# A delta-rule recurrence with a soft mixture of experts on one core: output tokens stored in runs of 20 a partition, 64-row remainders side by side, one urgency offset for each operation

## The chip, the cores and the metric

One core of a Trainium2 chip runs the whole program. The metric is the device time of one execution in microseconds. Three executions of the kernel before took 446.22, 451.45 and 451.5 us, median 451.45.

## The reference

```python
for t in range(S):                       # 4 batches, 8 heads, S = 768, D = 40
    y[:, :, t] = einsum('bhd,bhde->bhe', rt, state)
    Sa = einsum('bhde,bhe->bhd', state, at)
    state = state * wt[:, :, None, :] - einsum('bhd,bhe->bhde', Sa, bt)
    state = state + einsum('bhd,bhe->bhde', vt, kt)
x = y.transpose(0, 2, 1, 3).reshape(3072, 320)
logits = x @ phi                         # 32 slots, 4 for each of 8 experts
d = softmax(logits over the tokens)
slot_input = d.T @ x
for e in range(8):                       # w1[e]: 320 x 1024, w2[e]: 1024 x 320
    slot_out[e] = relu(slot_input[e] @ w1[e]) @ w2[e]
out = softmax(logits over the slots) @ slot_out
```

## The kernel before, in words

The sequence is cut into 12 steps of 64 tokens (`NST`), two of which make one superstep of 128. The 32 pairs of batch and head stand in three units (`u`) of 3, 3 and 2 heads. For a step, the decays `ww` are multiplied up by two scans on VectorE (`scan_s`, `scan_c`), which give the factors for `kb` (`scan_k`) and for `aa` (the product `ahs`). ScalarE spreads `ahs` into a block-diagonal matrix (`bd_mult`, for the first steps; later ones load it), with the mask column `bm_t`. `lgram` and `gram` multiply it with the keys on TensorE and mask the results. For each superstep a triangular matrix is inverted (`solve_in`, 30 `solve_step`, `solve_out`) by VectorE and GpSimd; it begins and ends with a transpose of 128 x 1024 on VectorE. With the inverse, `chain_g`, `chain_u` and `chain_s` carry the state from step to step, which is the serial part; `y_vut`, `y_sd`, `y_p` and `y_y` give the outputs `xs`. `slots_a` to `slots_e` turn them into logits, running maxima and sums, and the slots' inputs, which `merge_m` and `merge_s` finish as `sit`.

Then come the experts. In the first layer each output bank (experts 4g to 4g+3, half f of the 1024 columns) is filled by three passes over the 320 inputs: two of 128 rows and a remainder of 64 rows, four experts beside each other in the four column tiles of 32. ScalarE applies the ReLU, TensorE transposes, VectorE copies into `ht`. The second layer (`second`, 64 matmuls of 160 columns for each half of the output columns) adds into one bank. Its result is split into two float32r parts, combined by `sel_r`, and cast to `s4`. The last matmuls multiply the softmax over the slots, transposed by `stack` for each superstep, with `s4`: in groups of three, 160 columns each. ScalarE and VectorE copy the results out in turns, and SP stores them. Before, a partition holds token t of a step, so each run in memory is half a token's row, 640 bytes; the second half of the columns is computed while the first is stored.

No order is written out. Every call is recorded as an operation (`Plan.record`), with its cost by rules (`pe_cost`, `costs`), and `forward` lets each engine take, of the operations that are ready, the one with the highest urgency: the longest way to the end of the program, plus an offset. Before, the offsets are the sum of 32 random patterns (`noise`, `SEEDS`). Where the plan has TensorE wait over 0.9 us, `fill` puts filler matmuls, which stand under L550 (128 rows) and L554 (32 rows) in the profile. `pace` lets a transfer wait for an earlier one where over 500 KB would be in flight (`PACE`). All other planned instructions stand under one line, L1273 (L1276 after the change; the fillers under L553 and L557). In the profile `wt` stands for eight large tiles that the weights `in_w` share with the recurrence, `mem`, `old` and `mid` for smaller ones, `cs_t` for the constants.

## Time and profile before

| What | Value |
|---|---|
| median of three executions | 451.45 us (446.22 to 451.5) |
| span of the profiled execution | 443.0 us |
| median above that span | 8.45 us |
| busy: TensorE, VectorE, GpSimd, ScalarE | 376.9, 267.3, 242.8, 221.3 us |
| HBM read, written | 54.01 MB, 3.93 MB |

The page gives the profiled execution's span, from its first to its last instruction, and not its whole time; the fastest of the three executions is 3.2 us above this span. In a row of the timeline stand the start, the duration, the engine, the operation with its tiles and shape, and in brackets the idle time ahead of it with what ended it. A float32 matmul leaves two records. In the rows by stretches a pair of numbers is busy time and number of instructions.

### The profile page before, as it was taken

The numbers are of one execution on the slowest core, as the hardware profiler recorded it, in microseconds if no ns is written. First come the engines' busy times: TensorE is split into PE (matmuls) and PEld (weight loads), VectorE is DVE, ScalarE is ACT, GpSimd is POOL, SyncE is SP. The second block draws the span as 40 slices with busy tenths as digits, with TensorE's granted clock in tenths as the row PEclk, the third lists the DMA queues.
The fourth block names the chain that finished last, engine by engine and source line by source line (L and its number), as shares of the span: only waits on it lengthen the run. The fifth ranks groups of instructions, "written<-read, shape, count | busy, mean of one in ns | idle before, by whom it ended". The sixth has DMA issues, their size and how long they took to land.

```text
span 443.0 us, 21393 instructions
## 1 busy us (share of the span) xinstructions
PE 376.9 (85%) x9411; PEld 317.3 (72%) x9411; DVE 267.3 (60%) x554; ACT 221.3 (50%) x633; POOL 242.8 (55%) x410
## 2 busy tenths in 40 slices
PE   0497998998999899789998999989899887899900
PEld 0487997787978789678986789868787576537800
DVE  6869999789965377854479555646354542522400
ACT  1630364774555564957449854697257535202310
POOL 3838884897288964788976889278810000200000
PEclk9999999999999999999999999999899989979965
DMA  8997023135322334613446315585557835870276
GB/s 203 260 237 221 8 65 101 31 90 135 84 72 77 108 82 119 166 43 94 114 127 184 98 44 148 156 249 179 157 151 211 254 105 156 251 218 1 60 164 134
DMA packets 42206, 59.33 MB, mean 134 GB/s; under 512 B 4785, under 2 KB 32545, under 8 KB 42113
## 3 DMA queue, kind: packets, MB, share of 16 engines
q1 hardware_dynamic: 42113, 57.96, 47.3%
q8 instruction: 74, 1.21, 1.2%
q14 instruction: 19, 0.16, 0.1%
HBM read 54.01 MB, written 3.93 MB: 131 GB/s over the span
## 4 chain that ended last, share of the span: by engine, by line
PE 66%; DVE 8%; ACT 7%; DMA 6%; issue 4%; POOL 3%; SPq 1%; ACTq 0%; POOLq 0%; DVEq 0%
PE ps L1273 60%; DVE wt L1273 7%; ACT wt L1273 6%; POOL wt L1273 3%; PE ps L550 3%; PE ps L554 3%; DMA wt<-in_kb_dram 3%; DMA wt<-in_ww_dram 1%; DMA wt<-in_w_dram 1%; DVE mem L1273 1%; DMA wt<-in_aa_dram 1%; SPq L1273 1%; ACT mem L1273 1%; DMA wt<-in_rr_dram 0%; ACT mid L1273 0%
## 5 line engine op out<-in xcount | busy, mean ns | idle before, releaser
L1273 POOL TENSOR_TENSOR wt<-wt 128x30 f32<-128x30 f32 (+23 forms) x360 | 177.5, 493 | 58.7 <-ACT wt L1273 32.8
L1273 PE MATMUL ps<-wt,wt 128*32 128x40 f32 (+8 forms) x4200 | 134.3, 224 | 10.1 <-ACT wt L1273 4.0
L1273 PEld LDWEIGHTS ps<-wt,wt 128*32 128x32 f32 (+6 forms) x4200 | 114.4, 118 | 25.1 <-issue 8.1
L1273 DVE TENSOR_TENSOR wt<-ps,cs_t 128x384 f32<-128x384 f32 (+5 forms) x132 | 64.1, 498 | 49.3 <-PE ps L1273 39.0
L1273 PE MATMUL ps<-cs_t,wt 120*128 120x120 f32 (+5 forms) x496 | 69.0, 273 | 15.5 <-DMA cs_t<-in_consts_dram 13.3
L1273 ACT ACTIVATE wt<-ps 32x120 f32<-32x120 f32 (+1 forms) x288 | 70.1, 249 | 19.3 <-PE ps L1273 13.2
L1273 POOL TENSOR_TENSOR wt<-wt,wt 120x768 f32<-120x768 f32 x32 | 56.6, 1779 | 24.7 <-DVE wt L1273 8.7
L1273 ACT COPY wt<-ps 128x120 f32<-128x120 f32 (+3 forms) x116 | 38.9, 354 | 61.4 <-PE ps L1273 57.0
L1273 PEld LDWEIGHTS ps<-cs_t,wt 120*128 120x128 f32 (+5 forms) x496 | 52.2, 140 | 21.9 <-issue 14.8
L1273 PE MATMUL ps<-wt,mem 128*32 128x160 f32 (+4 forms) x592 | 65.2, 313 | 1.1 <-ACT mem L1273 0.4
L1273 ACT COPY mem<-ps 120x480 f32<-120x480 f32 (+6 forms) x99 | 45.0, 480 | 40.9 <-PE ps L1273 32.1
L1273 PEld LDWEIGHTS ps<-wt,mem 128*32 128x32 f32 (+4 forms) x592 | 52.5, 153 | 4.6 <-ACT mem L1273 1.6
L1273 DVE TENSOR_TENSOR_SCAN wt<-wt,wt 120x780 f32<-120x780 f32 x24 | 43.0, 1793 | 3.9 <-DMA wt<-in_ww_dram 2.1
L1273 DVE TENSOR_TENSOR wt<-wt 128x27 f32<-128x27 f32 (+25 forms) x100 | 41.4, 414 | 2.1
L1273 PE MATMUL ps<-mem 32*32 32x40 f32 (+2 forms) x1040 | 33.9, 232 | 3.4 <-issue 1.9
L1273 DVE TENSOR_TENSOR ps<-ps,wt 120x480 f32<-120x480 f32 (+1 forms) x30 | 18.1, 606 | 29.8 <-PE ps L1273 27.7
L1273 ACT ACTIVATE wt<-wt,bm_t 120x768 f32<-120x768 f32 (+1 forms) x36 | 28.5, 858 | 10.6 <-PE ps L1273 4.1
L1273 POOL MEMSET mem<- 128x2048 f32 x1 | 1.8, 1805 | 57.5 <-DVE mid L1273 57.5
L550 PE MATMUL ps<-cs_t 128*128 128x128 f32 x218 | 27.1, 280 | 1.1 <-ACT mem L1273 1.1
L1273 PE MATMUL ps<-wt 32*32 32x40 f32 x1536 | 24.6, 201 | 3.3 <-issue 1.3
L1273 ACT COPY wt<-wt 120x768 f32<-120x768 f32 (+5 forms) x20 | 16.5, 836 | 21.4 <-DVE wt L1273 18.8
L550 PEld LDWEIGHTS ps<-cs_t 128*128 128x128 f32 x218 | 25.6, 194 | 1.6 <-ACT mem L1273 1.3
(89 smaller groups left out, 323.1 us busy)
## 6 DMA issues: line engine op xcount, KB each, us to landing
wt<-in_w_dram SPq DMA_DIRECT2D x16, 640.0 KB
wt<-in_kb_dram SPq DMA_DIRECT2D x36, 240.0 KB
wt<-in_w_dram SPq DMA_DIRECT2D x16, 512.0 KB
wt<-in_ww_dram SPq DMA_DIRECT2D x12, 366.6 KB
...
```

Of the source, the lines that this page charges most:

```text
L550: self.nc.tensor.matmul(bank, src, src, start=True, stop=True)
L554: self.nc.tensor.matmul(bank[i:i + 32], src[r, 0:32], src[r], start=True, stop=True)
L1273: nc.vector.memset(one_f, 0.0)
```

## The change

Four things change together.

1. `stack` writes the transposed softmax of the first five supersteps into one tile `cst_old` of 2,560 columns, in the order batch, step, token. The last matmul takes every 20th column of it (`src[:, r::nr]`), so that partition q gets tokens 20q to 20q + 19; the last superstep gives 4 consecutive tokens a partition. A token's 320 columns come in one matmul, one copy for each, and a store moves 2 to 6 tokens of 32 partitions in runs of 2,560 to 7,680 bytes (24 stores; before, 20). Both halves of the second layer are therefore computed ahead of the first output, and `more`, which mixed them, is gone.
2. The loop over the first layer has `f` outside. Two banks (g = 0, 1) take the 128-row passes, then both remainders follow as one operation (`gather`): `w1_load` puts the remainders of experts 4 to 7 into the other half of the partitions, so that the eight matmuls stand in eight different tiles of 64 rows by 32 columns.
3. The offsets come from a table with one character for each operation (`SHIFT`).
4. The planner's costs: 16 array tiles for the matmuls instead of 4 columns, and the start of a matmul operation by kind (`START`) instead of 170; an operation may need two banks.

```diff
@@ -37,9 +37,8 @@
             ba=(0.824, 1.778), lw=(0.869, 1.012), br=(0.72, 0.82), s0=(0.643, 1.33))
 KV = 3
 BM, AV = NST, 2
-OX = ((1, 3, 7), (3, 7))
-OXG = ()
-FIN = dict(st=(0.03, 0.429), pos=(6, 0, 1), warm=(0, 0, 1, 1, 0, 1, 0, 0, 2, 0, 0), ms=(5, 2), l2=(6, 2, 3))
+OX = (2, 5, 10, 16, 20)
+FIN = dict(st=(0.03, 0.429), pos=(6, 0, 1), warm=(0, 0, 1, 1, 0, 1, 0, 0, 2, 0, 0), ms=(5, 2))
...
+START = ((225, 210), (195, 195))
 ROUNDS = 0
-SEEDS = (3, 21, 44, 62, 119, 136, 146, 166, 184, 236, 383, 839, 894, 1144, 1277, 1468, 1487, 1602, 1732, 2303, 3675, 4128,
-         4356, 4549, 5379, 5493, 5729, 5909, 5921, 5968, 6052, 6159)
-SPARE = 3
...
+STEP = {**{chr(79 + v): v for v in range(-44, 46)}, "~": 13, "!": -45}
+SHIFT = (
+    r"To')E:@oFhXL;s4JO+UO>!OQ!i0IXai!OO0zcwufU0#!2HOO,:!JPOTvYRS|N~[;tR7NkW~!7z]u2Hzu_O&B|%~!R_gLQOXOS#!OF|CO:H6NNQ!c"
...
+)
...
-            if o.mode == mode and isinstance(out, VAP) and o.banks == {out.bank} and o.tag == self.tag:
+            if o.mode == mode and isinstance(out, VAP) and (o.banks == {out.bank} or self.gather and o.gather) and o.tag == self.tag:
                 new = False
...
-            o.occ = self.pe_add(o, cost, lane) + 170
+            o.occ = self.pe_add(o, cost, lane) + START[method == "transpose"][mode[1] < 128]
...
-        for o, x in zip(self.ops, sum((self.noise(n) for n in SEEDS), 0 * self.noise(0))):
-            o.prio += x
+        for o, c in zip(self.ops, "".join(SHIFT)):
+            o.prio += 300 * STEP[c]
...
@@ -680,7 +683,8 @@
             for k in range(2):
                 nc.sync.dma_start(wv[:, 2 * p + k], w1[2 * i + p, 128 * k:128 * k + 128])
         for p in range(2):
-            nc.sync.dma_start(wv[64 * p:64 * p + 64, 4], w1[2 * i + p, 256:320])
+            o = 64 * ((p + i // 2) % 2)
+            nc.sync.dma_start(wv[o:o + 64, 4], w1[2 * i + p, 256:320])
 
     def w2_load(i, p):
         wv = wts[4 + i].rearrange("p (e j c) -> p e j c", e=2, c=HD)
@@ -1195,8 +1199,7 @@
             nc.vector.tensor_tensor(xv[:, :, 2:4], cb, xv[:, :, 0:2], ALU.subtract)
             for j in range(4):
                 nc.tensor.transpose(tp[:, 128 * j:128 * j + 128], x[:, 128 * j:128 * j + 128], ident)
-            t = cst_t[i] = stk[i]
-            (nc.vector.tensor_copy if i % 2 else nc.scalar.copy)(t, tp)
+            (nc.vector.tensor_copy if i % 2 else nc.scalar.copy)(stk[i], tp.rearrange("p (a b t) -> p a b t", a=2, t=C))
 
         mg = {}
 
@@ -1371,7 +1374,9 @@
                 w2_load(0, 1)
                 w2_load(1, 0)
         i = NSS - 1
-        stk += old_later([512] * (NSS - 1))
+        cst_old = old_later([512 * (NSS - 1)])[0]
+        ov = cst_old.rearrange("p (b s t) -> p b s t", b=B, t=C)
+        stk += [ov[:, :, 2 * k:2 * k + 2].rearrange("p b a t -> p a b t") for k in range(NSS - 1)]
         run_all(*y_lists(NST - 1, WIN), ([lambda k=k: slots_a(i, k, 0) for k in range(3)], .3, .6),
                 (one(lambda: stack(0)) + one(lambda: stack(1)), *FIN["st"]))
         w2_load(1, 1)
@@ -1385,7 +1390,7 @@
             seq.insert(x, lambda k=k: stack(k))
         for k, f in enumerate(seq):
             f()
-    rnd = mid_later([512, 256, 320, 320, 160, 160])
+    rnd = mid_later([512, 256, 320, 320, 320])
     w1s = [t.rearrange("p (a f) -> p a f", f=FF) for t in wts[:4]]
     w2s = [t.rearrange("p (e j c) -> p e j c", e=2, c=HD) for t in wts[4:]]
 
@@ -1396,24 +1401,32 @@
             nc.gpsimd.tensor_scalar(sel_r[:, k, :, b], sel.unsqueeze(1).broadcast_to([128, 2, NSL]), float(b == k), None,
                                     ALU.mult)
     sel_r = sel_r.rearrange("p k a b s -> p k (a b s)")
-    stk.append(rnd[0])
+    stk.append(rnd[0].rearrange("p (b a t) -> p a b t", b=B, t=C))
     o = 4 * HD + NG * C
     hs = mem[:, o:o + 2 * FF].rearrange("p (g f) -> p g f", g=2)
     ht = mem[:, 0:2048].rearrange("p (j e g s) -> p j e g s", j=8, e=4, g=2)
     nc.gpsimd.memset(ht, 0.0)
-    for g in range(2):
-        for f in range(2):
-            hp = bank("pa_a")
-            for k in range(3):
-                for eq in range(4):
-                    e = 4 * g + eq
-                    o = slice(32 * eq, 32 * eq + 32)
-                    p = e % 2
-                    r = slice(0, 128) if k < 2 else slice(64 * p, 64 * p + 64)
-                    wk = 2 * p + k if k < 2 else 4
-                    nc.tensor.matmul(hp[o], sit[r, k], w1s[e // 2][r, wk, 512 * f:512 * f + 512],
-                                     start=(k == 0), stop=(k == 2))
-            nc.scalar.activation(hs[:, g, 512 * f:512 * f + 512], hp, AF.Relu)
+    for f in range(2):
+        hps = [bank("pa_a") for _ in range(2)]
+
+        def first(g, k):
+            for eq in range(4):
+                e = 4 * g + eq
+                p = (e + g) % 2
+                r = slice(0, 128) if k < 2 else slice(64 * p, 64 * p + 64)
+                wk = 2 * (e % 2) + k if k < 2 else 4
+                nc.tensor.matmul(hps[g][32 * eq:32 * eq + 32], sit[r, k], w1s[e // 2][r, wk, 512 * f:512 * f + 512],
+                                 start=(k == 0), stop=(k == 2))
+
+        for g in range(2):
+            for k in range(2):
+                first(g, k)
+        nc.gather = True
+        for g in range(2):
+            first(g, 2)
+        nc.gather = False
+        for g in range(2):
+            nc.scalar.activation(hs[:, g, 512 * f:512 * f + 512], hps[g], AF.Relu)
             tp = bank("pt_a")
             for j in range(4):
                 nc.tensor.transpose(tp[:, 128 * j:128 * j + 128],
@@ -1426,58 +1439,42 @@
                     tp.rearrange("p (j x) -> p j x", j=4)[:, :, 32 * eq + c:32 * eq + c + 4])
     stack(NSS - 1, wts[2][:, 0:512])
 
-
-    ov = out.rearrange("(bh bl s t) c -> bl t s bh c", bh=2, bl=2, t=C)
     HC = HD // 2
-    sos = {}
-
-    def second(hf, x):
-        if x == 0:
-            sos[hf] = bank("pa_a")
-        g, j = divmod(x, 8)
-        for eq in range(4):
-            nc.tensor.matmul(sos[hf][32 * eq:32 * eq + 32, 0:HC], ht[:, j, eq, g],
-                             w2s[2 * g + eq // 2][:, eq % 2, j, HC * hf:HC * hf + HC], start=(x == 0), stop=(x == 15))
-
-    rest = [lambda x=x: second(1, x) for x in range(16)]
-
-    def more(n):
-        for _ in range(min(n, len(rest))):
-            rest.pop(0)()
-
-    for x in range(16):
-        second(0, x)
+    s4 = rnd[4]
     for hf in range(2):
-        if hf == 1:
-            more(16)
-        so = sos[hf]
-
+        so = bank("pa_a")
+        for x in range(16):
+            g, j = divmod(x, 8)
+            for eq in range(4):
+                nc.tensor.matmul(so[32 * eq:32 * eq + 32, 0:HC], ht[:, j, eq, g],
+                                 w2s[2 * g + eq // 2][:, eq % 2, j, HC * hf:HC * hf + HC], start=(x == 0), stop=(x == 15))
         sp = rnd[2 + hf].rearrange("p (k c) -> p k c", k=2)
         nc.scalar.copy(sp[:, 0], so[:, 0:HC])
         nc.vector.tensor_tensor(sp[:, 1], so[:, 0:HC], sp[:, 0].bitcast(F32), ALU.subtract)
-        more(FIN["l2"][0])
         sr = bank("pt_a")
         for k in range(2):
             nc.tensor.matmul(sr[:, 0:HC], sel_r[:, k], sp[:, k], start=(k == 0), stop=(k == 1))
-        s4 = rnd[4 + hf]
-        nc.scalar.copy(s4, sr[:, 0:HC])
-        more(FIN["l2"][1])
-        ot = wts[hf][:, 0:4 * NSS * HC]
-        for x in range(8):
+        nc.scalar.copy(s4[:, HC * hf:HC * hf + HC], sr[:, 0:HC])
+    tok = out.rearrange("(b n) c -> b n c", b=B)
+    heads = 2 * C * (NSS - 1)
+    ro, rm = heads // 32, 4
+    parts = [(cst_old, ro, tok[:, 0:heads], [wts[0][:, 0:16 * HD], wts[1][:, 0:(ro - 16) * HD]], OX),
+             (rnd[0], rm, tok[:, heads:], [wts[1][:, (ro - 16) * HD:(ro - 16 + rm) * HD]], (rm,))]
+    n = 0
+    for src, nr, dst, homes_, cuts in parts:
+        at = 0
+        for r in range(nr):
+            ot, x = (homes_[0], r) if r < 16 else (homes_[1], r - 16)
             op = bank("pt_a")
-            for t in range(3):
-                i, j = divmod(3 * x + t, 4)
-                nc.tensor.matmul(op[:, HC * t:HC * t + HC], cst_t[i][:, 128 * j:128 * j + 128], s4, start=True, stop=True)
-            (nc.vector.tensor_copy if x % 2 else nc.scalar.copy)(ot[:, 3 * HC * x:3 * HC * x + 3 * HC], op[:, 0:3 * HC])
-            more(FIN["l2"][2])
-            if x in OX[hf]:
-                k = OX[hf].index(x)
-                s0, s1 = (3 * (OX[hf][k - 1] + 1) // 2 if k else 0), 3 * (x + 1) // 2
-                for bl in range(2):
-                    for bh in range(2):
-                        (nc.gpsimd if 2 * bl + bh in OXG else nc.sync).dma_start(
-                            ov[bl, :, s0:s1, bh, HC * hf:HC * hf + HC],
-                            ot[64 * bl:64 * bl + 64].rearrange("p (s b c) -> p s b c", b=2, c=HC)[:, s0:s1, bh])
+            nc.tensor.matmul(op[:, 0:HD], src[:, r::nr], s4, start=True, stop=True)
+            (nc.vector.tensor_copy if n % 2 else nc.scalar.copy)(ot[:, HD * x:HD * x + HD], op[:, 0:HD])
+            n += 1
+            if r + 1 in cuts:
+                y = x + 1 - (r + 1 - at)
+                for b in range(B):
+                    nc.sync.dma_start(dst[b].rearrange("(q r) c -> q (r c)", r=nr)[:, HD * at:HD * (r + 1)],
+                                      ot[32 * b:32 * b + 32, HD * y:HD * (x + 1)])
+                at = r + 1
     nc.emit()
```

What it does to the order, at three places. First the start of the program, on SP, whose rows are the loads; `ww`, `aa` and `b` belong to steps 0 and 1 in turns, each of 360 KB, a `kb` load is 240 KB. Before:

```order
L1273 DMA wt_70<-in_ww_dram 120x782 x2
L1273 DMA wt_74<-in_aa_dram 120x768 x2
L1273 DMA wt_76<-in_b_dram 120x768
L1273 DMA mem<-in_b_dram 120x768
L1273 DMA bm_t<-in_consts_dram 120x3
L1273 DMA cs_t<-in_consts_dram 128x451
L1273 DMA wt_70<-in_kb_dram 120x512 x3
```

With the change:

```order
L1276 DMA wt_70<-in_ww_dram 120x782
L1276 DMA wt_74<-in_aa_dram 120x768
L1276 DMA wt_76<-in_b_dram 120x768
L1276 DMA wt_70<-in_ww_dram 120x782
L1276 DMA wt_74<-in_aa_dram 120x768
L1276 DMA wt_70<-in_kb_dram 120x512 x2
L1276 DMA bm_t<-in_consts_dram 120x3
L1276 DMA wt_70<-in_kb_dram 120x512
L1276 DMA mem<-in_b_dram 120x768
L1276 DMA wt_70<-in_kb_dram 120x512 x2
L1276 DMA cs_t<-in_consts_dram 128x451
L1276 DMA wt_70<-in_kb_dram 120x512
```

Step 0's w, a and b come first now; the constants `cs_t` follow behind five `kb` loads. ScalarE in the same place, where the six `ACTIVATE` rows are `bd_mult` of both steps (`wt_71`: step 0). Before:

```order
L1273 COPY wt_73<-wt_70 120x768
L1273 COPY old<-ps_61 128x2x120
L1273 COPY old<-ps_62 128x2x120
L1273 COPY wt_73<-wt_70 120x768
L1273 COPY old<-ps_63 128x2x80
L1273 COPY old<-ps_64 128x2x120
L1273 COPY old<-ps_65 128x2x120
L1273 COPY old<-ps_66 128x2x80
L1273 ACTIVATE wt_71<-wt_74,bm_t 120x768 x2
L1273 ACTIVATE wt_71<-wt_74,bm_t 120x512
L1273 ACTIVATE wt_77<-wt_74,bm_t 120x512
L1273 ACTIVATE wt_77<-wt_74,bm_t 120x768 x2
```

With the change:

```order
L1276 COPY wt_73<-wt_70 120x768
L1276 ACTIVATE wt_71<-wt_74,bm_t 120x768 x2
L1276 ACTIVATE wt_71<-wt_74,bm_t 120x512
L1276 COPY wt_73<-wt_70 120x768
L1276 ACTIVATE wt_77<-wt_74,bm_t 120x768 x2
L1276 ACTIVATE wt_77<-wt_74,bm_t 120x512
L1276 COPY old<-ps_66 128x2x120
```

Step 0's spreading is now ahead of step 1's copy and of the copies out of `ps`. VectorE does step 0's product `ahs` ahead of step 1's second scan, and in the superstep behind it `solve_out` ahead of the next `solve_in`.

Second, SP where the data of step 10 are loaded (`in_vq`, `in_rr`, `in_vv`), behind a run of weight loads `in_w`. Before:

```order
L1273 DMA wt_73<-in_w_dram 128x1024
L1273 DMA wt_73<-in_w_dram 64x1024 x2
L1273 DMA mem<-in_vq_dram 128x320
L1273 DMA wt_77<-in_rr_dram 40x256
L1273 DMA wt_76<-in_vv_dram 32x1280
L1273 DMA wt_77<-in_rr_dram 40x256 x3
L1273 DMA wt_76<-in_vv_dram 32x1280
```

With the change:

```order
L1276 DMA wt_70<-in_w_dram 128x1024
L1276 DMA wt_73<-in_w_dram 64x1024 x2
L1276 DMA mem<-in_vq_dram 128x320
L1276 DMA wt_77<-in_rr_dram 40x256
L1276 DMA wt_75<-in_w_dram 128x4x320
L1276 DMA wt_72<-in_w_dram 128x1024
L1276 DMA wt_72<-in_w_dram 64x1024
L1276 DMA wt_72<-in_w_dram 128x1024
L1276 DMA wt_72<-in_w_dram 64x1024
L1276 DMA wt_77<-in_rr_dram 40x256
L1276 DMA wt_76<-in_vv_dram 32x1280 x2
```

The two `in_vv` loads now stand behind five more loads of weights. Third, TensorE in the first expert layer (`sit`), at the remainders and what follows. Before:

```order
L1273 MATMUL ps_67<-wt_70,sit 32x512 x2
L1273 MATMUL ps_67<-wt_71,sit 32x512 x2
L1273 MATMUL ps_61<-wt_70,sit 32x512 x2
L1273 MATMUL ps_61<-wt_71,sit 32x512 x2
L1273 MATMUL ps_68<-wt_72,sit 32x512 x2
L1273 MATMUL ps_68<-wt_73,sit 32x512 x2
L1273 MATMUL ps_66<-wt_72,sit 32x512 x2
L1273 MATMUL ps_66<-wt_73,sit 32x512 x2
L1273 MATMUL ps_63<-cs_t,mem 128x128 x4
L1273 MATMUL ps_64<-cs_t,mem 128x128 x4
```

With the change (remainders of the first half of the columns):

```order
L1276 MATMUL ps_62<-wt_70,sit 32x512 x2
L1276 MATMUL ps_62<-wt_71,sit 32x512 x2
L1276 MATMUL ps_65<-wt_72,sit 32x512 x2
L1276 MATMUL ps_65<-wt_73,sit 32x512 x2
L1276 MATMUL ps_64<-cs_t,wt_72 128x128 x4
L1276 MATMUL ps_63<-cs_t,mem 128x128 x4
L1276 MATMUL ps_68<-cs_t,mem 128x128 x4
L1276 MATMUL ps_61<-wt_70,sit 32x512 x2
```

Before, the remainders of four banks followed each other, and the transposes of `hs` (`cs_t,mem`) came behind them all; now the remainders of two banks alternate and the transposes follow directly.

75 lines of the change are left out of this document (40 added, 35 removed).

## The prediction

> **What bounds the kernel now.** I read the page first (span, busy time, chain), then a table of stretches, then the two ends of the program in order of time, since the change has named work at both ends and only reorders the middle.
>
> ```profile
> span 443.0 us, 21393 instructions
> PE 376.9 (85%) x9411; PEld 317.3 (72%) x9411; DVE 267.3 (60%) x554; ACT 221.3 (50%) x633; POOL 242.8 (55%) x410
> ...
> PE 66%; DVE 8%; ACT 7%; DMA 6%; issue 4%; POOL 3%; SPq 1%; ACTq 0%; POOLq 0%; DVEq 0%
> ```
>
> TensorE carries two thirds of the chain. The stretches show where it does not (time and count for each engine, then granted clock, DMA share, GB/s):
>
> ```profile
> core 0: us, PE busy (x) PEld busy (x) DVE busy (x) ACT busy (x) POOL busy (x), PEclk, DMA share, GB/s
> 0.00:20.00 20.00, 3.03 (x24) 2.61 (x28) 16.45 (x16) 7.48 (x14) 11.99 (x9) 1.00 0.90 228
> 20.00:40.00 20.00, 18.60 (x452) 17.27 (x448) 14.45 (x37) 6.47 (x14) 10.89 (x28) 1.00 0.97 248
> 40.00:60.00 20.00, 18.60 (x373) 17.93 (x365) 19.39 (x29) 6.45 (x13) 18.28 (x25) 1.00 0.21 56
> ...
> 422.00:443.00 21.00, 0.00 (x0) 0.00 (x0) 0.00 (x0) 0.43 (x1) 0.00 (x0) 0.56 0.68 148
> ...
> ```
>
> Until 20 us TensorE is idle. From 40 to 60 it is busy, but with fillers, while VectorE has 19.39 of 20 us of real work: the first triangular solve. From 422 us on one copy of 0.43 is all that is computed and stores run alone, at a DMA share of 0.68. So three limits follow each other: loads and VectorE, then TensorE, then stores.
>
> **The change, part by part.** The sum is made against the profiled span, 443.0 us; the median of the runs shown is 8.45 above it, and I carry the sum over to the median.
>
> *Start.* The orders of SP and ScalarE (above) now bring step 0's data first. The rows of before:
>
> ```profile
> 4.71 1.78 DVE L1273 TENSOR_TENSOR_SCAN wt<-wt,wt 120x780 f32<-120x780 f32 x1 [2.10 <-DMA wt<-in_ww_dram]
> ...
> 12.51 7.09 DVE L1273 TENSOR_TENSOR wt<-wt,wt 120x768 f32<-120x768 f32 x3
> ...
> 26.30 2.09 DVE L1273 STREAM_TRANSPOSE wt<-wt 128x1024 f32<-128x1024 f32 x1
> 28.31 0.91 DVE L1273 TENSOR_TENSOR wt<-wt,wt 120x768 f32<-120x768 f32 x1
> ```
> ```profile
> 10.96 3.11 POOL L1273 TENSOR_TENSOR wt<-wt,wt 120x768 f32<-120x768 f32 x1 [6.27 <-DMA wt<-in_b_dram]
> 14.03 2.38 POOL L1273 TENSOR_TENSOR mem<-mem,wt 120x768 f32<-120x768 f32 x1
> ```
> ```profile
> 13.32 1.30 PE L1273 MATMUL ps<-cs_t,wt 120*128 120x120 f32 x6 [13.32 <-DMA cs_t<-in_consts_dram]
> ...
> 19.60 1.94 PE L1273 MATMUL ps<-wt,wt 120*32 120x96 f32 x48 [2.74 <-ACT wt L1273]
> ...
> 23.80 1.63 PE L1273 MATMUL ps<-wt,mem 120*32 120x96 f32 x48
> ...
> ```
> ```profile
> 10.55 0.83 ACT L1273 COPY wt<-wt 120x768 f32<-120x768 f32 x1 [4.58 <-DVE wt L1273]
> ...
> 17.09 4.64 ACT L1273 ACTIVATE wt<-wt,bm_t 120x768 f32<-120x768 f32 x6
> ```
>
> The first `lgram` (19.60) waits for ScalarE's `bd_mult`, which starts at 17.09 because VectorE did both steps' scans before the first `ahs` product. The loads arrive in the order of issue: w of step 0 by 4.71, b of step 0 (fifth, 1,813 KB in) by 10.96, the constants (2,400 KB in) by 13.32, so some 235 KB a microsecond. In the new order b of step 0 is third (1,087 KB: 7.8), w of step 1 fourth (9.3), `bm_t` comes at 12.9, b of step 1 at 15.5, the constants at 18.5. Then, with the scans at 1.78: scan 6.5, small operations 7.0, second scan 8.7, scan of step 1 9.3 to 11.1, `ahs` product 2.36 (a third of 7.09) to 13.5, three `bd_mult` (half of 4.64) to 15.8: `lgram` of step 0 there, where it was at 19.60. Step 1: 0.4 of small operations and a scan to 15.7, product to 18.1, `bd_mult` to 20.4 (GpSimd's product, 15.5 and 2.38, is done at 17.9). So `lgram` of step 1 starts 3.4 us earlier than 23.80. If the two products take 0.91, as the one at 28.31, it is 18.4, a lead of 5.4 (there `bm_t` at 12.9 sets the first `bd_mult` and ScalarE's 0.83 copy comes between). The constants' 5 us of delay cost nothing: the first mask is wanted behind 15.8 + 1.9, and the transposes that used them go behind the solve's inputs. I take **−4.4**. VectorE keeps the lead, since it is full until 60 us.
>
> The fillers bear on this. The planner puts them where it has TensorE wait; one filler is four matmuls on 32 rows (eight records) or one on 128 (two records):
>
> ```profile
> 36.73 3.70 PE L554 MATMUL ps<-cs_t 32*32 32x128 f32 x128 [0.96 <-issue]
> ...
> 48.36 5.31 PE L550 MATMUL ps<-cs_t 128*128 128x128 f32 x46
> ```
>
> 3.70/16 and 5.31/23 both give 0.231 us for one. In the first 165 rows of TensorE's order the program had 140 and now has 128, 2.8 us less; behind them 44 and 36. I take 2.8 as the lower end of the lead. Also `solve_out` of the first solve now stands ahead of the next solve's `solve_in`, so the transposed inverse is there one transpose (2.09) sooner; as VectorE's total is the same, I take half, **−1.0**, with 0 and −2.1 as ends.
>
> *Middle.* From about 120 to 390 us the same matmuls, copies and solves run in another order. I cost this at nothing: where TensorE is full an order of the same work moves no end, and the eight fillers fewer there (1.8 us) speak for no loss. What it costs if that fails, and wins if it does better, are the first and the last rival.
>
> *First expert layer.* A pass is four column tiles:
>
> ```profile
> 399.88 0.13 PEld L1273 LDWEIGHTS ps<-wt,sit 64*32 64x32 f32 x4 [0.30 <-issue]
> ...
> 400.31 0.13 PEld L1273 LDWEIGHTS ps<-wt,sit 64*32 64x32 f32 x4 [0.30 <-issue]
> ...
> 402.57 1.97 PE L1273 MATMUL ps<-cs_t,mem 128*128 128x128 f32 x16
> ...
> 402.70 0.60 ACT L1273 ACTIVATE mem<-ps 128x512 f32<-128x512 f32 x1 [0.26 <-PE ps L1273]
> ...
> 404.90 7.54 PE L1273 MATMUL ps<-wt,mem 128*32 128x160 f32 x216
> ```
>
> They follow at 0.43. The 64-row remainders are eight passes; side by side they are four, 1.7 us less. But the transposes of `hs` now follow each half directly: behind the second half TensorE waits for a 0.60 ReLU with two handovers (0.7) and for a second (0.1), behind the first some 0.4 in all. Net −0.5, or +1.2 if two row groups don't run together, which no row here shows. I take **0**. The Trainium skill, TensorEngine Tiling (Array Packing), Restrictions and Gotchas, says that row tiles must write different PSUM banks; the change gives each half its own, so by it the −0.5 would hold.
>
> *Second layer and stores.* Before, the first half's output was stored while the second half was computed; now both halves come first. 256 records at 7.54/216 are 8.9 us. Then the handover to the first store:
>
> ```profile
> L1273 DVE COPY wt<-ps 128x480 f32<-128x480 f32 x8 | 5.0, 653 | 4.4 <-PE ps L1273 4.2
> ...
> L1273 ACT CAST mid_r<-ps 128x160 fp32r<-128x160 f32 x4 | 1.2, 292 | 9.8 <-PE ps L1273 9.8
> L1273 DVE COPY mem<-ps 128x16 f32<-128x16 f32 x10 | 1.1, 166 | 0.0
> ...
> L1273 DVE TENSOR_TENSOR mid_r<-ps,mid_r 128x160 fp32r<-128x160 f32 x2 | 0.6, 324 | 6.1 <-ACT mid_r L1273 6.1
> ```
>
> Cast, difference, combine and cast: 0.29 + 0.32 + 0.45 + 0.29 with handovers, 1.6. The first store takes six tokens, three copies on VectorE; 653 ns for 480 columns and 166 for 16 give 0.485 for 320, so 1.5, with matmul and handovers 1.9. Sum 12.4, where 404.90 to the first store at 416.03 was 11.1: **+1.3**. Now the stores themselves:
>
> ```profile
> L1273 SPq DMA_DIRECT2D out_dram<-wt x20: 595/596/710, 416.0 to 438.9; - x20
> ```
> ```profile
> L1273 SPq DMA_DIRECT2D wt<-in_vv_dram x24: 311/316/1483, 21.6 to 356.2; - x24
> ```
> ```profile
> SPq L1273 <- DMA out_dram<-wt: 10.3, 12, 1.3
> ```
> ```profile
> 428.00:438.00 10.00, 0.00 (x0) 0.00 (x0) 0.00 (x0) 0.00 (x0) 0.00 (x0) 0.50 0.74 161
> ```
>
> In twelve places SP waits 0.86 on the mean (10.3/12) for an earlier store: the planner's limit of 500 KB in flight lets in two stores of 240 KB. Issue to landing is thus 2 × (0.596 + 0.86) = 2.9. At 161/0.74 = 218 GB/s a store moves in 1.13, so 1.2 is fixed. A new store is 32 partitions with one run each, like the loads of `in_vv`, whose issue takes 0.316. Then a 240 KB store lands after 0.32 + 1.2 + 1.13 = 2.65, two in flight: 1.33 each, 185 GB/s; of 160 KB after 2.27, three in flight: 216 GB/s. The six largest (1.39 MB) take 7.5, the rest (2.54 MB) 11.8, the last landing 1.5 and the end 1.1: 21.9. The same sum for before (eight stores at 0.64, 1.0 of waiting for copies, twelve at 1.46, 1.5 and 1.1) gives 26.2, where 27.0 were measured, so 22.7, a gain of 4.3. With an issue of 0.6 it is 2.0; at the loads' rate (248/0.97 = 256 GB/s) 5.7. I take **−4.2**, since shape says more of the issue than direction. The copies hide: 18 more on two engines are 4.5 us beneath 22.
>
> Sum: −4.4 − 1.0 + 0 + 1.3 − 4.2 = −8.3; span 434.7, median **443.2**. The ends add to 439 and 449.
>
> **The rivals.**
> *Slower: weight loads ahead of step 10's data* (chance 0.12).
>
> ```profile
> 274.65 35.54 SPq L1273 DMA_DIRECT2D wt<-in_w_dram  x17
> ```
> ```profile
> 309.08 4.76 DMA wt<-in_w_dram
> ...
> 315.94 2.16 DMA wt<-in_rr_dram
> ```
>
> SP's run of 17 weight loads cost 2.1 us a load, and the chain went through its end. Now five further weight loads stand ahead of the two `in_vv` loads of step 10: 10.4 us. TensorE has 29 fillers there, 6.7 us, and little else. If the lead of 5.4 is eaten and the loads come 10.4 late: 451.45 − 2.9 + 10.4 = 459. From a wait of 8.3 us on it decides the sign. Against it: fillers behind the start became fewer, not more.
> *The lead is lost* at that wait: only the stores' −2.9 is left, 448.6 (0.18).
> *The stores are no quicker* (0.12): 451.45 − 5.4 + 1.3 = 447.4. For it speaks that rows of 640 bytes already move at 218 of some 256 GB/s, against it SP's 10.3 us of waiting. The Trainium skill, DMA: Bandwidth & Descriptors, Specifications, puts the shortest transfer for full rate at 512 bytes, so by it longer rows win nothing; the 218 against 256 agree only nearly.
> *The reordered middle gains as well* (0.20): the offsets touch every operation.
>
> ```profile
> 340.00:360.00 20.00, 17.06 (x321) 12.92 (x320) 12.06 (x37) 10.09 (x33) 0.00 (x0) 0.91 0.69 213
> 360.00:380.00 20.00, 17.32 (x499) 15.37 (x500) 5.17 (x12) 8.23 (x25) 0.00 (x0) 1.00 0.50 147
> 380.00:400.00 20.00, 17.91 (x182) 7.74 (x174) 6.03 (x25) 2.98 (x10) 3.16 (x5) 0.83 0.70 214
> ```
>
> These three have 7.7 us of idle TensorE beside 1.8 of fillers saved; some 7 of it gives 436. For it speaks that the copies' transposes (`stack`) now fill the last slots' waits; against it that these are waits of a chain, which no order shortens.
>
> **How the numbers follow.** My forecast has 0.38 and 443.2 us, alone 439 to 449. With the rivals the range is 434 to 453: it leaves out the worst of the slower case and the best of the middle. Faster by over 2% (about what a measurement of this kernel can tell from no change) means under 442.4: nearly all of the reordered middle (0.19), somewhat under half of the forecast (0.17) and a little of the two rivals with smaller gains (0.04), 0.40. Slower by over 2%, over 460.5: half of the first rival, 0.06. Within: 0.54.
>
> **What would show it.** Right: the first `solve_in` transpose at 21 to 23, not 26.30; `out_dram` issues of 0.32 and a rate over 180 GB/s while stores run alone; first layer to second layer about 14.4 us as before; store start 12.4 us behind the second layer's. Wrong: an issue of 0.6 again, the stores at 160 GB/s, a TensorE gap of 8 us and more ahead of step 10's `chain_g`, or the lead gone by 180 us.

## The result, and the profile after

| | median | lowest to highest | span of the profiled execution |
|---|---|---|---|
| before (4 executions) | 451.17 us | 446.22 to 451.5 | 443.0 |
| with the change (4) | 429.35 us | 428.65 to 431.43 | 426.9 |

The ratio is 0.957, interval 0.951 to 0.963: 4.3% faster, where 443.2 us was forecast and 434 to 453 given. Ratios leave out executions more than 1.5% above the fastest of their kernel; medians and ranges hold all of them.

The page of the changed kernel:

```profile
span 426.9 us, 21521 instructions
PE 365.3 (86%) x9473; PEld 312.1 (73%) x9473; DVE 261.7 (61%) x558; ACT 221.6 (52%) x637; POOL 246.7 (58%) x410
...
PE 60%; DVE 11%; ACT 8%; POOL 7%; issue 7%; DMA 3%; SPq 1%; DVEq 0%; ACTq 0%
```

TensorE has 11.6 us less of busy time, fillers included, for the same work, and carries a smaller part of the chain. To see where the 16.1 us between the two spans come from, cut both traces at the same events: the transposes that end the second solve, the one that ends the last, the first matmul of each expert layer, the first store (us):

| stage | before | after | difference | forecast |
|---|---|---|---|---|
| to the second solve's transposes | 117.1 | 111.8 | -5.3 | -5.4 |
| to the last solve's | 209.5 | 200.4 | -9.1 | 0 |
| to the first expert layer | 63.9 | 66.5 | +2.6 | 0 |
| first layer, to the second | 14.4 | 14.6 | +0.2 | 0 |
| second layer, to the first store | 11.1 | 12.6 | +1.5 | +1.3 |
| stores, to the end | 27.0 | 21.0 | -6.0 | -4.2 |

*Start.* TensorE, then ScalarE and VectorE, in order of time:

```profile
15.76 1.93 PE L1276 MATMUL ps<-wt,wt 120*32 120x96 f32 x48 [15.76 <-ACT wt L1276]
17.44 3.24 PE L557 MATMUL ps<-mem 128*32 128x128 f32 x56
20.43 1.29 PE L1276 MATMUL ps<-wt,mem 120*32 120x96 f32 x48
```
```profile
13.24 2.37 ACT L1276 ACTIVATE wt<-wt,bm_t 120x768 f32<-120x768 f32 x3 [3.90 <-DMA bm_t<-in_consts_dram]
15.52 0.81 ACT L1276 COPY wt<-wt 120x768 f32<-120x768 f32 x1
16.25 2.37 ACT L1276 ACTIVATE wt<-wt,bm_t 120x768 f32<-120x768 f32 x3
```
```profile
22.50 2.10 DVE L1276 STREAM_TRANSPOSE wt<-wt 128x1024 f32<-128x1024 f32 x1
...
64.41 3.93 DVE L1276 STREAM_TRANSPOSE wt<-wt 128x1024 f32<-128x1024 f32 x2
...
111.82 4.07 DVE L1276 STREAM_TRANSPOSE wt<-wt 128x1024 f32<-128x1024 f32 x2
...
312.18 2.00 DVE L1276 STREAM_TRANSPOSE wt<-wt 128x1024 f32<-128x1024 f32 x1 [2.23 <-POOL wt L1276]
```

The two `lgram` start at 15.76 and 20.43 (forecast 15.8 and 20.4), the first solve at 22.50 instead of 26.30. But ScalarE has spread step 1 by 18.62; what its `lgram` waits for is the fillers that TensorE began at 17.44. Of VectorE's rows the last two are events of the table.

*Middle.* The stretch between the second and the last solve, before and after (one row each of the view by stretches), and the fillers in it:

```profile
117.14:326.60 209.46, 197.87 (x5546) 169.94 (x5547) 128.80 (x246) 125.74 (x378) 157.65 (x262) 0.99 0.44 124
```
```profile
111.82:312.18 200.36, 189.82 (x5259) 163.04 (x5257) 125.07 (x241) 127.67 (x382) 165.89 (x263) 0.99 0.42 124
```
```profile
L550 PE MATMUL ps<-cs_t 128*128 128x128 f32 x60 | 7.1, 277 | 0.0
L554 PE MATMUL ps<-cs_t 32*32 32x128 f32 (+1 forms) x168 | 5.6, 269 | 1.0 <-ACT wt L1273 1.0
```
```profile
L553 PE MATMUL ps<-cs_t 128*128 128x128 f32 x50 | 5.8, 275 | 0.0
L557 PE MATMUL ps<-cs_t 128*32 128x128 f32 x8 | 0.4, 285 | 0.0
```

The stretch is 9.1 us shorter and TensorE is busy 8.05 us less. Its time there and in the next stretch, own work first, then the fillers where they do not overlap it, then idle time (us):

| stretch | own work | fillers | idle |
|---|---|---|---|
| second to last solve, before | 186.4 | 11.5 | 11.6 |
| second to last solve, after | 184.0 | 5.9 | 10.5 |
| last solve to first layer, before | 50.2 | 5.1 | 8.6 |
| last solve to first layer, after | 49.8 | 9.0 | 7.7 |

In the first stretch there are 25 fillers fewer, in the second 15 more; fillers and idle time together fall from 23.1 to 16.4 and rise from 13.6 to 16.7. So part of the gain is given back behind the last solve, and over both stretches 6.5 us are left. In the first stretch one group of fillers stands at the second solve's transposes in both kernels (6.3 us at 117.2 before, 5.75 at 111.6 now). Before, six more stood later (at 132.6, 181.0, 185.3, 190.7, 235.2 and 293.0), five of them in waits of the chain of the state, for VectorE's transposed inverse or ScalarE's copies in `chain_u`; now there is only one, 0.43 us at 225.8.

*First expert layer and stores.* TensorE in order of time, then SP's store issues (least, median and longest in ns), its waits, and a stretch in which only stores run:

```profile
378.65 6.36 PE L1276 MATMUL ps<-wt,sit 128*32 128x512 f32 x48 [0.36 <-DVE sit L1276]
...
386.77 4.66 PE L1276 MATMUL ps<-wt,sit 128*32 128x512 f32 x48
392.19 1.15 PE L1276 MATMUL ps<-cs_t,mem 128*128 128x128 f32 x8 [0.76 <-ACT mem L1276]
393.27 8.90 PE L1276 MATMUL ps<-wt,mem 128*32 128x160 f32 x256
```
```profile
L1276 SPq DMA_DIRECT2D out_dram<-wt x24: 314/315/429, 405.9 to 423.9; - x24
```
```profile
SPq L1276 <- DMA out_dram<-wt: 9.1, 15, 1.8
```
```profile
410.00:422.00 12.00, 0.00 (x0) 0.00 (x0) 0.61 (x2) 0.00 (x0) 0.00 (x0) 0.64 0.85 205
```

The issue fell from 0.596 to 0.315 us, the DMA share while stores run alone rose from 0.74 to 0.85 and the rate from 161 to 205 GB/s. The second `hs` transposes wait 0.76 for the ReLU.

### The profile page after: what moved, and what is told of

It reads as the page before. It is cut to its first block, busy times and chain, and to the rows that moved or that the text cites. A ratio compares the mean times of both kernels' runs of the same rounds, so it can differ in the third digit from the quotient of the medians.

```text
span 426.9 us, 21521 instructions
## 1 busy us (share of the span) xinstructions
PE 365.3 (86%) x9473; PEld 312.1 (73%) x9473; DVE 261.7 (61%) x558; ACT 221.6 (52%) x637; POOL 246.7 (58%) x410
## 4 chain that ended last, share of the span: by engine, by line
PE 60%; DVE 11%; ACT 8%; POOL 7%; issue 7%; DMA 3%; SPq 1%; DVEq 0%; ACTq 0%
PE ps L1276 53%; DVE wt L1276 9%; POOL wt L1276 7%; ACT wt L1276 5%; PE ps L557 4%; DMA bm_t<-in_consts_dram 2%; PE ps L553 2%; ACT mem L1276 2%; DMA mem<-in_rr_dram 1%; SPq L1276 1%; DVE mem L1276 1%; DVE old L1276 0%; DVE ps L1276 0%; ACT mid L1276 0%; DVE old_r L1276 0%
## 5 line engine op out<-in xcount | busy, mean ns | idle before, releaser
L1276 POOL TENSOR_TENSOR wt<-wt 128x30 f32<-128x30 f32 (+23 forms) x360 | 182.0, 506 | 53.3 <-ACT wt L1276 27.4
L1276 PE MATMUL ps<-wt,wt 128*32 128x40 f32 (+9 forms) x4200 | 136.7, 225 | 22.9 <-ACT wt L1276 15.9
L1276 PEld LDWEIGHTS ps<-wt,wt 128*32 128x32 f32 (+7 forms) x4200 | 116.2, 118 | 36.7 <-issue 24.8
L1276 DVE TENSOR_TENSOR wt<-ps,cs_t 128x384 f32<-128x384 f32 (+6 forms) x132 | 63.4, 496 | 34.1 <-PE ps L1276 30.3
L1276 ACT COPY mem<-ps 120x512 f32<-120x512 f32 (+6 forms) x99 | 46.0, 483 | 37.4 <-PE ps L1276 33.4
L1276 PE MATMUL ps<-wt,mem 128*32 128x160 f32 (+4 forms) x592 | 62.2, 305 | 0.0
L1276 DVE TENSOR_TENSOR wt<-wt 128x27 f32<-128x27 f32 (+25 forms) x100 | 38.8, 388 | 2.0
L1276 PEld LDWEIGHTS ps<-wt 32*32 32x32 f32 x1536 | 19.2, 109 | 13.1 <-issue 5.8
L1276 DVE STREAM_TRANSPOSE wt<-wt 128x1024 f32<-128x1024 f32 x12 | 24.6, 2095 | 2.4 <-POOL wt L1276 2.2
L1276 PEld LDWEIGHTS ps<-mem 32*32 32x32 f32 (+2 forms) x1040 | 18.8, 108 | 9.0 <-issue 4.3
(91 smaller groups left out, 314.4 us busy)
```

The source lines that it names most:

```text
L1276: nc.vector.memset(one_f, 0.0)
```

## The experiments

The stages of the table above (us; in the last column the median, behind it that of before on the same chip). Left out are e1, which is before again, e7, e10 and e13, profiled in an execution with a mean granted clock of only 0.93, and e9, whose first stages are the change's. In e4 the planned instructions stand under L1332, in e17 under L1335.

| run | second solve | last solve | first layer | layer | first store | stores | time |
|---|---|---|---|---|---|---|---|
| e2 middle | 110.8 | 199.4 | 66.4 | 12.9 | 11.1 | 27.9 | 434.1 / 450.1 |
| e3 end | 120.1 | 214.9 | 62.1 | 15.6 | 12.6 | 21.5 | 445.0 / 450.1 |
| e4 start | 117.4 | 209.7 | 68.8 | 15.5 | 11.1 | 27.1 | 451.9 / 450.1 |
| e5 rest | 121.8 | 199.4 | 66.7 | 15.3 | 11.1 | 27.0 | 442.5 / 448.9 |
| e6 cut | 117.7 | 204.1 | 65.7 | 14.6 | 11.1 | 27.1 | 445.6 / 448.9 |
| e8 zero | 120.3 | 200.0 | 81.5 | 15.5 | 12.8 | 21.4 | 459.0 / 448.9 |
| e18 before, zero | 122.2 | 207.3 | 74.2 | 14.9 | 11.1 | 26.8 | 462.9 / 447.1 |
| e11 more fillers | 115.2 | 198.5 | 67.4 | 13.4 | 12.6 | 21.0 | 430.6 / 450.2 |
| e12 not side by side | 113.2 | 201.8 | 68.1 | 15.7 | 12.6 | 21.0 | 433.6 / 450.2 |
| e14 more in flight | 112.3 | 200.7 | 68.4 | 14.4 | 12.6 | 17.4 | 428.4 / 447.9 |
| e15 e11 + e14 | 117.7 | 197.4 | 66.2 | 13.4 | 12.6 | 17.3 | 425.5 / 447.9 |
| e16 the change | 115.0 | 201.6 | 67.8 | 12.9 | 12.6 | 21.0 | 432.8 / 448.3 |
| e17 no fillers, e14 | 113.2 | 205.1 | 62.7 | 14.3 | 12.6 | 17.5 | 424.2 / 448.3 |

**The base.** The kernel before, unchanged.

> The kernel before, unchanged, for the base of the sum. The prediction carried a gain from the span of one execution (443.0 us) to a median 8.45 us above it; with the change the executions lie 1.74 to 1.83 above their own spans. Theory: what lies around the span is the same here, so spans of 444.5 to 449.8 belong to the times of 446.2 to 451.5, and the profiled execution of before was simply a quick one: its time was near 444.8. Rival: the spans repeat near 443 and 8 us lie around them, so that the change took 6 us out of what lies around the span.

450.5 us, ratio 0.998 (0.992 to 1.004). All 35 executions of before on this chip lie 1.7 to 1.9 us above their own spans; they run from 443.95 to 456.33. So the profiled execution, span 443.0, took about 444.8 by this distance, and the 8.45 us of the prediction were no constant around the span but mostly the distance of a quick execution from the median. The times go with the mean granted clock of TensorE: 0.942 to 0.968, correlation -0.87, 3.9 us for each hundredth; which of the two causes the other is not shown by that.

**Which half.** The first 2,476 operations are the same in both kernels. e2 gives them the changed costs and offsets and keeps the old end; e3 keeps costs and offsets of before and takes the new end (`OLD` is before's table of offsets).

```diff
+        off[:2476] = [300 * STEP[c] for c in "".join(SHIFT)[:2476]]   (e2, with START and the 16 tiles)
+        off[:2476] = OLD                                              (e3, with 170 and 4 columns)
```

> Offsets and planner's costs of the change for the first 2476 operations, the same in both kernels; the first expert layer, the second and the stores as before. Each engine's order is the changed kernel's up to the first expert layer. Theory (the reordered middle and the start carry most): the first layer starts 11 to 12 us earlier than at 390.46, and the time is 434 to 440. Rival of the prediction (the middle at nothing, only the start's 4.4 + 1.0): 446. Rival (everything is the stores): 451.

> The other half: order and costs of before for these 2476 operations, with the changed first layer, second layer and stores. Theory, from the two traces (first layer to the end 52.5 us before, 48.25 after): 4.3 us less, 446.9. The prediction's own terms, +1.3 and -4.2, gave 2.9 less, 448.3. If stores and order help each other (the planner sees the stores' way to the end), the two halves do not add to the change's 21.8 us.

e2: 434.1 us, ratio 0.967 (0.959 to 0.976). e3: 445.0, ratio 0.994 (0.989 to 0.999). By the medians 16.0 and 5.1 us add to 21.1, by the ratios 3.3% and 0.6% to 3.9%, where the change has 4.3%: within the intervals the halves add, and the order is three quarters of the gain or more. e2 lies in its theory's range; e3 cannot tell 4.3 us from the prediction's 2.9. From the first layer on e3 takes 49.7 us where before takes 52.6: 2.9 less, the prediction's own figure, with 1.2 us more in a first layer at a lower clock.

**Which part of the order.** In e4 to e6 each engine's order is written out (`TURNS`) and put together from the two: the changed first 62 us and before's rest; the reverse; the changed first 225 us and before's rest.

```diff
+        turns = {e: [self.ops[x // 5] for x in TURNS if x % 5 == k] for k, e in enumerate(engs)}
-                for o in cand[e]:
+                for o in [x for x in turns[e][:1] if x in cand[e]]:
```

> Before, with each engine's order written out: the 350 operations that the changed kernel plans for its first 62 us stand in the changed order, all others behind them in the order of before. Theory of the prediction: a lead of 4.4 to 5.4 us at the first solve that nothing takes away: 446 to 447, the first transpose of a solve at 21 to 23 us. Rival (the lead is lost at later waits, and the middle's own order makes the gain): 450 to 452, with the lead gone before 180 us.

> The counterpart of the run on the start: each engine's order written out, the first 65 us of the plan in the order of before, all later operations up to the first expert layer in the changed order, the end as before. The start alone gave nothing (451.9 against 450.1), start and middle together 16 us (434.1). Theory A (the middle's own order makes the gain, whatever stands ahead of it): 435 to 438. Theory B (the two belong together: an order made for one start is of little use behind another): 443 to 450.

> The changed order for what the changed kernel plans for its first 225 us (four of six solves), the order of before behind it. In the two traces the lead at the transposes grew from 3.8 us at the first solve to 5.3, 8.4, 11.3, 12.1 and 14.4 us at the others. Theory A (the gain is made stretch by stretch): a lead near 11 us at the fifth solve that stays, 439 to 441. Theory B (it is one late place, step 10's loads or the last solve): 448 to 451.

e4: 451.9 us, ratio 1.005 (0.999 to 1.012): the start alone is worth nothing, as the rival had it. Its VectorE rows, and those of before:

```profile
23.90 2.12 DVE L1332 STREAM_TRANSPOSE wt<-wt 128x1024 f32<-128x1024 f32 x1
...
67.09 4.02 DVE L1332 STREAM_TRANSPOSE wt<-wt 128x1024 f32<-128x1024 f32 x2
```
```profile
66.80 2.07 DVE L1273 STREAM_TRANSPOSE wt<-wt 128x1024 f32<-128x1024 f32 x1
69.03 2.11 DVE L1273 STREAM_TRANSPOSE wt<-wt 128x1024 f32<-128x1024 f32 x1
```

Of 2.4 us at the first solve 1.9 are left at `solve_out` (67.09 against 69.03), but the second solve begins at 69.1, where it began at 66.80: `solve_out` ahead of `solve_in` costs the next solve a transpose. At the second solve's transposes e4 is level with before (117.4 and 117.1). In the change, too, the second solve begins only 0.5 us sooner than before (66.26); its lead of 5.3 us at the end comes from a second solve of 45.6 us instead of 50.3.

e5: 442.5, ratio 0.985 (0.979 to 0.991). At its seam, where the two orders are joined, it is 4.6 us behind (121.8), yet after it the stretch takes 199.4 as in the change. e6: 445.6, 0.994 (0.988 to 1.000). Though it has the changed order there, it is not ahead at the second solve (117.7); it leads by 3.6 us at the third (174.5 against 178.06) and by 6.1 at the fourth, and loses 2.6 again behind its seam. Neither time lies in theory A's range, and e5's lies just short of theory B's; what speaks for theory A is the stretch itself. It takes 197.4 to 201.8 in the kernels that have the changed order there, whatever start stands ahead (e2, e5, e11, e12, e14, e15, e16 and the change), 209.5 to 214.9 in those with before's (before, e3, e4). Fillers and idle time of TensorE together are 15.5 to 17.9 us of it in the first group, 23.1 to 27.4 in the second. The clock is not the reason: with the same 3.4 us at half clock in this stretch it takes 209.5 and 209.7 (before, e4) against 200.4 and 200.7 (the change, e14). The lead of the start is not as firm: kernels with the whole changed order come to the second solve's transposes at 110.8 to 117.7. Which engine's order it is was not tried.

**Costs or offsets.** e8 is the change with all offsets at zero, e10 before with only the changed costs, e18 before with all offsets at zero.

```diff
-            o.prio += 300 * STEP[c]
+            o.prio += 0 * STEP[c]          (e8)
-        for o, x in zip(self.ops, sum((self.noise(n) for n in SEEDS), 0 * self.noise(0))):
-            o.prio += x                    (e18)
```

> The changed kernel with every offset at zero: the planner's own urgencies, its changed costs and the changed end. Theory A (the table of offsets is what makes the order good): the five microseconds of the end are all that is left, 446 or slower. Theory B (the changed costs make the order good and the table is a detail): 430 to 434.

> Before, with only the planner's changed costs (16 array tiles, starts by kind) and the offsets of before. Theory (costs and offsets have to fit each other, as the all-zero table at 459 suggests): 449 to 458, no gain. Rival (the costs describe the chip better and give a better order by themselves): 435 to 443.

> Before, with every offset at zero: its own costs, its own end. With the changed costs and all offsets at zero the stretch between the transposes of the second and the last solve took 200.0 us, as with the table (200.4), and with the changed costs and before's offsets 207.1; before takes 209.5 to 214.9. Theory A (before's offsets made the middle slow, the plain urgencies do it in 200 under either costs): 200 to 203 us there, and a long last stage (80 us and more from the last solve to the first layer) that puts the time at 455 or above. Theory B (the changed costs make the middle quick): 208 or more there.

e8: 459.0 us, ratio 1.014 (1.007 to 1.022). e10: 477.0, 1.051 (1.044 to 1.059). e18: 462.9, 1.037 (1.031 to 1.043). Without offsets the changed costs have the middle in 200.0 us, before's costs in 207.3, so e18's first theory fell, and the second missed by little; both lose more behind the last solve (81.5 and 74.2 us to the first layer). Work can be moved across the last solve, so the two stages have to be added: 281.5 under either costs without offsets, 273.4 to 278.5 with before's offsets (before, e3, e4), 265.8 to 269.9 with the table (e2, e12, e14, e16, the change). So the changed costs do not do it without the table, and under the old offsets they are the worst of all, beyond what e10's theory had. The table under before's costs was not run; whether it needs the changed costs stays open.

**Fillers and the clock.** e7 leaves out before's fillers planned between 70 and 390 us, e13 those of the changed order; e11 has 27 more of them in the changed order. Fillers compute nothing that is used.

```diff
-            if o.at < first:
+            if o.at < first or 70e3 < o.at < 390e3:      (e7, e13, e17)
-FILL = (900, 500, 225)
+FILL = (500, 250, 225)                                   (e11, e15)
```

> Before, without the fillers that stand in the plan between 70 and 390 us (some 50 of them, 11 to 12 us of TensorE at 0.231 us each); they compute nothing that is used. Theory A (the fillers stand where TensorE has real work ready on the chip, so the order gains by having fewer): 440 to 444. Theory B (they only fill waits of the chain, so fewer fillers are a sign of the gain and not its cause): 449 to 452, with about as much more idle time on TensorE; the granted clock may change too.

> The changed kernel's order, written out, with fillers in planned waits from 0.5 us on and 0.25 us left open (before: 0.9 and 0.5): 191 instead of 164 fillers, 6.2 us more of them. Theory A (a wait of TensorE costs twice, itself and a stretch of 3.5 us and more at half clock behind it): fewer such stretches, granted clock 0.97 or more, 426 to 429. Theory B (in this order the fillers stand in front of real work): 431 to 436.

> The changed kernel's order, written out, without the fillers that the plan has between 70 and 390 us; they compute nothing that is used. In before's order the same step lowered the granted clock from 0.957 to 0.931 and cost 5 us. Theory A (the changed order has real work in the waits behind the solves: between the second and the last solve it has 58 filler records where before had 232): clock 0.950 to 0.960, 431 to 435, and 200 to 204 us between the solves' transposes at 112 and 312. Theory B (the changed order lives on its fillers like the other): clock 0.94 or less, 436 to 440, and over 206 us there.

e7: 454.7 us against 448.9, ratio 1.006 (0.999 to 1.013), clock 0.914 to 0.942 where before has 0.942 to 0.972. e11: 430.6, ratio 0.956, clock 0.966 to 0.980. e13: 426.1, ratio 0.953 (0.944 to 0.962), clock 0.929 to 0.951. e7's theory A, a gain, fell. More fillers raise the clock and fewer lower it, but the time does not follow: e11 gains nothing by its 0.98, e7 loses little, and e13, for which both theories had a slower kernel than the change, comes out no slower. Medians of before differ by up to 3 us from chip to chip, so the change ran again (e16) beside the last version, e17 (below): in the profiled executions e17 is 5.5 us ahead, 3.5 by its stores and 5.1 from the last solve to the first layer, 62.7 us instead of 67.8. There the change has

```profile
318.79 1.16 PE L553 MATMUL ps<-cs_t 128*128 128x128 f32 x8 [1.55 <-DVE mem L1276]
...
320.49 3.25 PE L557 MATMUL ps<-cs_t 32*32 32x128 f32 x111
...
325.52 3.46 PE L557 MATMUL ps<-cs_t 128*32 128x128 f32 x120
```

Those are 7.9 us of fillers in the waits of the last chain; e17 waits 1.68, 3.58 and 1.79 us in their place and is through 1.2 us sooner (12.6 against 13.9 us from the last transposes to the `32x40` matmuls behind these waits). The other 3.9 of the 5.1 us come later, where e16 has four pauses of TensorE, 4.4 us together, that end with nothing the trace shows, and e17 one of 0.9; why is not shown. In the middle, without fillers and at half clock for 20 us, e17 is 3.5 us slower (205.1 against 201.6). So in these two traces the fillers pay in the middle and hold the chain up a little at the end.

**First layer.** e12 puts both banks' remainders into the same half of the partitions; every instruction stands where it stood.

```diff
-            o = 64 * ((p + i // 2) % 2)
+            o = 64 * p
-                p = (e + g) % 2
+                p = e % 2
```

> The changed kernel with the 64-row remainders of both banks in the same half of the partitions, so that the second four of each eight follow the first four; every instruction stands where it stood. Theory (side by side saves half of eight passes of 0.43 us): first to second layer 14.62 + 1.7 = 16.3 us, 431. Rival (the remainders hide behind each other's start and the weight loads anyway): 14.6, 429.4.

433.6 us, ratio 0.963 (0.957 to 0.970). Its TensorE:

```profile
383.06 7.00 PE L1276 MATMUL ps<-wt,sit 128*32 128x512 f32 x48 [0.36 <-DVE sit L1276]
...
391.45 5.49 PE L1276 MATMUL ps<-wt,sit 128*32 128x512 f32 x48
```

The second half takes 5.49 instead of 4.66: 0.83 for four passes of 0.43 less two, so 1.7 for both halves, as the first theory had it (the first halves differ in their clock too, and the time of the whole kernel is too coarse to show it). So two row groups do run together. The Trainium skill, TensorEngine Tiling (Array Packing), Restrictions and Gotchas, asks for different PSUM banks for that; over each column tile the change's two row tiles have them (not each half as a whole, as the prediction put it), and these 0.83 us agree. The layer as a whole is where it was: 12.9 us in e2 with the old one and in e16 with the new, both first halves at full clock.

**Stores.** e9 cuts each store into its two halves of columns, so that runs are 640 bytes again on 32 partitions; e14 lets 1,400 KB of stores be in flight.

```diff
+                    for h in range(2):
+                        nc.sync.dma_start(dst[b].rearrange("(q r) c -> q r c", r=nr)[:, at:r + 1, HC * h:HC * h + HC], ...
-        most = PACE[3] if n > PACE[2] else PACE[0]
+        most = PACE[3] if n > PACE[2] or o.n > 2476 else PACE[0]
```

> The changed kernel with each store cut into its two halves of 160 columns: 48 stores instead of 24, the same 32 partitions, but runs of 640 bytes again. It separates what made the stores quicker (21.0 us from the first issue to the end, 27.0 before). Theory A (long runs allow the short issue: 0.315 us for one run a partition, 0.6 for several): issues of about 0.6 us, 48 of them 28.8 us, so the end comes 9 us later, 438. Theory B (32 partitions make the issue short and 640-byte rows are as quick): issues of 0.315, 15 us in all, the end at most 2 us later, 429 to 431. Theory C (the rows themselves are slower at 46 ns for 640 bytes): issue short, but the rate back at 160 to 170 GB/s, 433 to 435.

> The changed kernel's order, with 1,400 KB of stores in flight instead of 500. SP waited 9.1 us in 15 places for earlier stores; the stores moved at 205 GB/s with the DMA queues 0.86 busy. Theory A (the queues are short of work): the end 2 to 3 us sooner, 426.5 to 428, share 0.95 and more. Theory B (the queues are full enough, 237 GB/s is what rows of any length reach): within 1 us of 429.4.

e9: 440.2 us, ratio 0.978 (0.975 to 0.982). e14: 428.4, 0.960 (0.951 to 0.968), its stores 17.4 us instead of 21.0. The issues and a stretch of stores alone of e9, then of e14:

```profile
L1276 SPq DMA_DIRECT2D out_dram<-wt x48: 316/438/708, 410.4 to 435.3; - x48
```
```profile
414.00:434.00 20.00, 0.00 (x0) 0.00 (x0) 0.00 (x0) 0.00 (x0) 0.00 (x0) 0.56 0.63 146
```
```profile
411.00:421.00 10.00, 1.59 (x7) 1.36 (x6) 2.33 (x6) 1.40 (x4) 0.00 (x0) 0.67 0.89 261
```

In e9 SP waits 0.2 us for stores in all: it only issues, 48 times, mostly at 0.44 (2 to 6 runs for each of 32 partitions) and eight times at 0.6 (four whole runs, which merge into 128 of 640 bytes). That is theory A with a smaller price, and it rules out theory B. In e14 no store waits for another any more, and 261 GB/s are moved at a share of 0.89: the stores are 3.6 us shorter, a little more than theory A had. The time, 428.4, lies within 1 us of the change's all the same, as theory B had it, since the stretch from the last solve to the first layer took about 2 us longer in the profiled execution. Length has little to do with it: e9's records of 640 bytes and the change's of 2,560 to 7,680 move 15.0 bytes alike in a nanosecond of their time (before's 13.8).

**What the runs point to.** e15 is e14 with e11's fillers; e16 is the change again; e17 is e14 without fillers from 70 us on.

> The wider limit for the stores together with the fillers from 0.5 us on (that run had a clock of 0.98 and the same time as the change). Theory A (both hold): 425 to 428 and a smaller spread than the change's. Theory B (neither does): 429 to 431.

> The changed kernel once more, unchanged, on the same chip as the next run, because the medians of before differ by 2 us between chips (447.9 to 450.2) and the last differences are of that size. Without such a difference: 427 to 431.

> The changed order without the fillers between 70 and 390 us and with 1,400 KB of stores in flight. Theory A (the two gains add: the fillers' absence gave 3.3 us, the stores 3.6 in the trace): 420 to 424, granted clock 0.93 to 0.95. Theory B (the lower clock takes it back, as it took 5 us in the order of before): 426 to 431, with a wide spread.

e15: 425.5 us, ratio 0.954 (0.947 to 0.961). e16: 432.8, 0.968 (0.957 to 0.979). e17: 424.2 (423.25 to 427.2), 0.951 (0.942 to 0.960): the fastest, 2.0% below the change on the same chip. Its median is 8.6 us below e16's. e15 lies in the range of its first theory, e17 at the edge of its. The change itself came out above the 427 to 431 us expected of e16; by both ratios its gain is 3 to 4%.

## Why the prediction was wrong

The span was forecast at 434.7 and came at 426.9; the other 6.0 of the 13.85 us are the base.

- **Start, -4.4 and -1.0.** The numbers came (15.8 and 20.4 at `lgram`, 5.3 of 5.4 at the second solve), in part by luck. Step 1's product `ahs` took 0.96 us on VectorE and not 2.36, and the arrival of `bm_t` set the first `bd_mult` (13.24); ScalarE had step 1 ready at 18.6, close to the 18.4 that the forecast had as its other end, and its `lgram` then stood up to 1.8 us behind fillers. The reason was wrong too: the lead does not carry by itself. In e4 it is used up by the swap of `solve_out` and `solve_in`, which the prediction booked as a gain of half a transpose, and which sends the second solve off a transpose later. In the change the second solve is 4.8 us shorter, which no term had.
- **Middle, "I cost this at nothing: where TensorE is full an order of the same work moves no end".** This is the step that failed. TensorE was not full: 11.5 us of fillers and 11.6 of idle time stood in the 209.5 us between the second and the last solve. The prediction had counted the fillers in the orders, eight fewer behind the start, 1.8 us; that is about the balance of 25 fewer in this stretch and 15 more behind it, and the trace could have said where they stand. The changed order has matmuls left for most of these waits, fillers and idle time fall by 6.7 us, and the stretch is 9.1 shorter. That these waits shrink is read off the traces; that the order is the cause is shown by e2 and e5. The prediction's middle reaches to the first layer, and up to there 2.6 us are given back: -6.5 where 0 was forecast. The rival of the reordered middle had the sign and, at 436 us and a chance of 0.20, came nearest, but its rows are those from 340 to 400 us, behind the last solve, where the change lost. There "these are waits of a chain, which no order shortens" was not refuted; the mistake was to look for waits only there. An order doesn't shorten such a wait but can fill it.
- **First expert layer, 0.** Right: +0.2, in it -1.7 for the remainders (twice e12's 0.83) and against it the waits for the ReLU, 0.76 of them seen in one row.
- **Start of stores, +1.3.** +1.5.
- **Stores, -4.2.** -6.0. Mechanism right (issue 0.315, no longer 0.596; 0.32 was forecast), size too small: the bare sum gave 21.9 us, the 0.8 by which the same sum missed before was added to it, and 21.0 were measured. The rule weighed there, the Trainium skill, DMA: Bandwidth & Descriptors, Specifications (512 bytes for full rate), agrees: longer rows did not move faster than e9's 640 bytes. It was no argument against the change, because the gain came from SP's issue and the waits behind it.
- **The base.** "The median of the runs shown is 8.45 above it, and I carry the sum over": e1 shows 1.8 us around each span. With the change the median is 2.45 above the profiled span. Where a slower execution of before's order loses its time, one trace shows: in e3 the stretch between the second and the last solve takes 214.9 us, with 10.2 of them at half clock, where the profiled execution of before had 209.5 and 3.4. So the traces compare the change with a quick execution of just the stretch that it shortens.
- **The slower rival**, weight loads ahead of step 10's data, did not come: TensorE's longest wait from 260 to 330 us is not for a load,

```profile
PE ps L553 <- DVE mem L1276: 2.1, 1, 2.1
```

  and only without the fillers does a load end a wait of over a microsecond there, 1.79 us for `in_vv` (e17).
